# Three token tiles of a second product, cut into column and row parts of the array

## The chip, the cores and the metric

The kernel runs on one core of one Trainium2 chip. Its engines are TensorE (PE; PEld in the profile is its weight load), VectorE (DVE), ScalarE (ACT), GpSimd (POOL) and SyncE (SP, which here issues nearly all DMAs). The metric is device time in microseconds; less is better.

## The reference

The input x has 2048 tokens of 1024 features, in bf16. Each token is normalised over its features, multiplied by w1 (1024 x 3584), given a bias and a tanh GELU, and multiplied by w2 (3584 x 1024) with a second bias:

```python
def reference(x, w1, b1, w2, b2):
    y = _layernorm(x, axis=-1)
    h = _gelu(jnp.einsum("bsd,df->bsf", y, w1) + b1)
    return jnp.einsum("bsf,fd->bsd", h, w2) + b2
```

## The kernel before

All weights and all of x are kept in SBUF. The tokens are worked through in four blocks of 512 (`TB`), each of four token tiles of 128; tiles 4 to 7 are the second block, which the code calls block 1. For every block there are two products.

The first product (`mm1_row`, whose matmuls are issued by `pe_cell`, line 415) makes 28 rows of h, transposed: each row r has 128 of the 3584 hidden features on the partitions and the block's 512 tokens along the free dimension. A row is eight matmuls of 128x512, accumulated in one PSUM bank, followed by one GELU on ScalarE (line 432) into `hT_sb[:, r, :]`. The first block's opening rows are done in pieces of 128 tokens.

The second product (`out_chunk`, line 453) takes one token tile and one half of the 1024 output features at a time. Such a group is 28 matmuls (line 466), one for each `ft`. The stationary operand is a 128x128 square of `hT_sb` (128 hidden features by 128 tokens), the moving operand is 128x512 of `w2_sb`, and the 28 products accumulate in one bank of `ps_2`. That tensor has two banks (`NB2`), which the groups use in turn: group g waits until group g - 2 has been evicted (`grp_oe[g - NB2]`). The eviction is one addition on VectorE (line 477) which adds the bias `b2_sb` and writes bf16 to `o_sb`; then SP issues a store (line 482) of 128 KB. `o_sb` has two buffers, used by the token tiles in turn. Block 1 has eight groups, two to each of the tiles 4 to 7. The very last group of the kernel is cut into four pieces of 128 columns.

The order on each engine is that in which the program is written: every engine has a list of operations (`_Prog`), and `_emit` writes it out, with a wait on a semaphore only where the awaited value is higher than one the engine has already waited for. TensorE's list is strictly: first product of a block, second product of it, first product of the next.

VectorE's list is merged from two by a small planner (lines 569 to 584). `crit` holds the evictions, each with the time at which its matmuls are estimated to end; `fill` holds the preparation of the next blocks (statistics, normalisation, and the 32x32 stream transposes of line 355 that turn x into `yT_sb`). An eviction is taken when its estimated time has come, else a piece of preparation. The planner sets the order only; at run time each operation waits for its semaphores. The transposes that stand between the evictions of block 1 are those of block 3.

## Time and profile before

| what | value |
|---|---|
| timed runs | 398.50 and 398.64 us, median 398.57 |
| span of the profiled execution | 396.9 us (the page gives no total for it) |
| timed median less that span | 1.67 us |
| TensorE matmuls | 2116, busy 394.1 us |
| matmul of 128x512 in the second product | 868, mean 379 ns |
| weight load of 128x128 | mean 98 ns |
| VectorE busy | 152.8 us |
| eviction of 128x512 on VectorE | 31, mean 692 ns |

Matmuls are pipelined: the 379 ns run from the start of one to the modelled end of its drain, while the next has begun. The pace is read from start to start, by a stretch of the chain and the number of matmuls in it. The granted clock is the share of TensorE's full clock that the throttle let through.

The second product of block 1 by tiles, each a stretch from the first matmul of the tile to the first of the next:

| tile | stretch, us | TensorE busy | VectorE busy |
|---|---|---|---|
| 4 | 152.95 to 165.04 | 12.09 | 11.15 |
| 5 | 165.04 to 177.12 | 12.08 | 10.97 |
| 6 | 177.12 to 189.21 | 12.09 | 9.24 |
| 7 | 189.21 to 201.29 | 12.08 | 1.38 |

### The profile page before, as it was taken

To read this page: it belongs to the slowest core of one execution; us is meant where nothing else is said; L and a number is where in the kernel's file an instruction comes from. 1 tells how busy PE (TensorE), PEld (TensorE's weight loads), DVE (VectorE), ACT (ScalarE), POOL (GpSimd) and SP (SyncE) were. 2 spreads that over 40 slices of the span, in tenths; PEclk is the share of its full clock that TensorE was granted. 3 is DMA by queue.
4 is the path that set the end of the run, shared out by engine and by line. 5 is a ranking of instruction groups with operands and counts; after the bars stand their busy time and mean duration, and the time that the engine had idled before them with its cause. 6 is when DMAs were issued, how large, how long until landed. Compare 5 with 4: busy or idle time off the path is not lost.

```text
span 396.9 us, 4883 instructions
## 1 busy us (share of the span) xinstructions
PE 394.1 (99%) x2116; PEld 191.7 (48%) x2116; DVE 152.8 (38%) x345; ACT 82.8 (21%) x124; POOL 9.7 (2%) x24
## 2 busy tenths in 40 slices
PE   9999999999999999999999999999999999999998
PEld 8944444444444444444444444444444444444447
DVE  5847899989998005988100000001100000001011
ACT  4273430000133442000024433100003334400000
POOL 2101000020002000000000000000000000000000
PEclk9999999999999999999999999999999999999999
DMA  8999940000000000000000000000000000000000
GB/s 286 347 380 384 387 154 13 26 29 13 26 2 0 2 0 1 28 13 26 28 13 0 2 0 2 13 13 28 16 24 15 0 0 2 0 13 28 13 28 26
DMA packets 16924, 23.64 MB, mean 60 GB/s; under 512 B 1672, under 2 KB 10504, under 8 KB 16904
## 3 DMA queue, kind: packets, MB, share of 16 engines
q1 hardware_dynamic: 16616, 22.95, 16.4%
q8 instruction: 16, 0.26, 0.3%
q10 hardware_dynamic: 288, 0.39, 0.3%
q14 instruction: 4, 0.03, 0.0%
HBM read 19.14 MB, written 4.19 MB: 59 GB/s over the span
## 4 chain that ended last, share of the span: by engine, by line
PE 99%; ACT 0%; DVE 0%; issue 0%
PE ps L466 49%; PE ps L415 41%; PE ps_t L415 8%; PE ps L490 1%; PE ps_t L378 0%; ACT yT_sb L385 0%; DVE o_sb L477 0%
## 5 line engine op out<-in xcount | busy, mean ns | idle before, releaser
L466 PE MATMUL ps<-w_sb,hT_sb 128*128 128x512 bf16 (+1 forms) x980 | 194.2, 361 | 0.0
L415 PE MATMUL ps<-yT_sb,w_sb 128*128 128x512 bf16 (+1 forms) x920 | 167.4, 340 | 0.1
L466 PEld LDWEIGHTS ps<-w_sb,hT_sb 128*128 128x128 bf16 x980 | 91.3, 98 | 102.7
L415 PEld LDWEIGHTS ps<-yT_sb,w_sb 128*128 128x128 bf16 x920 | 80.9, 98 | 82.5 <-issue 0.3
L432 ACT ACTIVATE hT_sb<-ps,b_sb 128x512 bf16<-128x512 f32 x94 | 64.0, 688 | 237.2 <-PE ps L415 217.1
L477 DVE TENSOR_TENSOR o_sb<-ps,b_sb 128x512 bf16<-128x512 f32 (+1 forms) x35 | 22.6, 646 | 198.2 <-PE ps L466 198.1
L355 DVE STREAM_TRANSPOSE yT_sb<-x_sb 32x256 bf16<-32x256 bf16 x192 | 83.7, 436 | 26.6 <-PE ps_t L415 23.5
L415 PE MATMUL ps_t<-yT_sb,w_sb 128*128 128x512 bf16 x144 | 34.0, 379 | 0.0
L264 DVE BATCH_NORM_STATS2 st_sb<-x_sb 128x6 f32<-128x512 bf16 x32 | 21.1, 674 | 4.9 <-DMA x_sb<-in_x_dram 4.9
L415 PEld LDWEIGHTS ps_t<-yT_sb,w_sb 128*128 128x128 bf16 x144 | 14.0, 98 | 16.8
L432 ACT ACTIVATE hT_sb<-ps_t,b_sb 128x512 bf16<-128x512 f32 x18 | 12.4, 690 | 17.0 <-PE ps_t L415 14.6
L425 DVE TENSOR_TENSOR ps<-ps,rbc_sb 128x256 f32<-128x256 f32 x24 | 9.7, 426 | 6.1 <-PE ps L415 5.9
L268 POOL TENSOR_TENSOR rstd_sb<-mv_sb,nhalf 128x1 f32<-128x1 f32 x16 | 8.9, 559 | 118.7 <-DVE mv_sb L271 118.7
L290 DVE TENSOR_SCALAR x_sb<-x_sb,mv_sb,rstd_sb 128x1024 bf16<-128x1024 bf16 (+1 forms) x15 | 7.8, 525 | 3.9 <-POOL rstd_sb L268 3.3
L385 ACT COPY yT_sb<-ps_t 128x512 bf16<-128x512 bf16 (+2 forms) x8 | 4.4, 545 | 8.1 <-PE ps_t L378 8.1
L490 PE MATMUL ps<-const-bfloat16-1.0 128*128 128x128 bf16 x40 | 4.6, 302 | 0.8 <-PEq L613 0.8
L490 PEld LDWEIGHTS ps<-const-bfloat16-1.0 128*128 128x128 bf16 x40 | 4.0, 139 | 1.0 <-issue 0.8
L271 DVE BATCH_NORM_AGGREGATE mv_sb<-st_sb 128x2 f32<-128x15 f32 x16 | 3.5, 221 | 1.3
L337 DVE STREAM_TRANSPOSE rbc_sb<-rq_sb 32x64 f32<-32x64 f32 x16 | 3.8, 236 | 0.2
L378 PE MATMUL ps_t<-ident,x_sb 128*128 128x128 bf16 x24 | 2.3, 219 | 0.0
L425 DVE TENSOR_TENSOR ps_t<-ps_t,rbc_sb 128x256 f32<-128x256 f32 x4 | 1.6, 405 | 0.1
L493 ACT ACT_TABLE_LOAD x1 | 1.3, 1283 | 1.7 <-PEq L613 1.7
(24 smaller groups left out, 8.0 us busy)
## 6 DMA issues: line engine op xcount, KB each, us to landing
w_sb<-in_w_dram SPq DMA_DIRECT2D x4, 1792.0 KB, 18.3
out_dram<-o_sb SPq DMA_DIRECT2D x31, 128.0 KB, 1.7
x_sb<-in_x_dram SPq DMA_DIRECT2D x3, 1024.0 KB, 14.1
w_sb<-in_w_dram SPq DMA_DIRECT2D x2, 1024.0 KB, 9.1
w_sb<-in_w_dram SPq DMA_DIRECT2D x1, 2048.0 KB, 15.2
w_sb<-in_w_dram SPq DMA_DIRECT2D x8, 224.0 KB, 4.7
w_sb<-in_w_dram SPq DMA_DIRECT2D x1, 1280.0 KB, 14.7
x_sb<-in_x_dram SPq DMA_DIRECT2D x5, 128.0 KB, 4.6
```

The costliest lines, as they stand in the source:

```text
L264: return (lambda e, i=i, h=h: e.bn_stats(st_sb[:, i, 6 * h:6 * (h + 1)], x_sb[:, i, h * HC:(h + 1) * HC]), [x_ev[i][h]], f"st{i}_{h}", 0.65)
L268: pool.op(lambda e, i=i: e.tensor_tensor(out=rstd_sb[:, i:i + 1], in0=mv_sb[:, i, 1:2], in1=nhalf[:, i:i + 1], op=ALU.pow), waits=[f"mv{i} ...
L290: return (lambda e, i=i, c0=c0, c1=c1: e.tensor_scalar(out=x_sb[:, i, c0:c1], in0=x_sb[:, i, c0:c1], scalar1=mv_sb[:, i, 0:1], scalar2=rst ...
L337: res.append((lambda e, src=src, dst=dst: e.transpose(out=dst, in_=src), [f"rq{N_CENTRED - 1}"], ("rbc" if tq == 3 and q == 3 else None), ...
L355: res.append((lambda e, src=src, dst=dst: e.transpose(out=dst, in_=src), waits, (f"tr{i}" if lastop else None), 0.47))
L385: act.op(lambda e, dst=dst, src=src: e.copy(out=dst, in_=src), waits=[f"tp{i}_{k}"], sig=f"te{i}_{k}")
L415: pe.op(lambda e, b=b, r=r, dt=dt, n0=n0, n1=n1, bank=bank: e.matmul(unit_bank(bank)[:, n0:n1], lhsT=w1_sb[:, dt, r * P:(r + 1) * P], rhs= ...
L425: crit.append((est[wait_ev], (lambda e, ap=ap: e.tensor_tensor(out=ap, in0=ap, in1=rbc_sb[:, :, :].rearrange("p t s -> p (t s)"), op=ALU.m ...
L432: act.op(lambda e, r=r, n0=n0, n1=n1, bank=bank: e.activation(out=hT_sb[:, r, n0:n1], in_=unit_bank(bank)[:, n0:n1], func=ACT.Gelu_apprx_tanh,
L466: pe.op(lambda e, st=st, ft=ft, c0=c0, c1=c1, bank=bank: e.matmul(ps_2[:, bank, 0:c1 - c0], lhsT=hT_sb[:, ft, st * P:(st + 1) * P], rhs=w2 ...
L477: crit.append((est[sig], (lambda e, ob=ob, c0=c0, c1=c1, bank=bank: e.tensor_tensor(out=o_sb[:, ob, c0:c1], in0=ps_2[:, bank, 0:c1 - c0], ...
L490: pe.op(lambda e: e.matmul(ps_1[:, 0, 0:P], lhsT=unit, rhs=unit, start=True, stop=True), waits=[gate] if gate else [])
```

## The change

Three token tiles of block 1's second product are computed with their matmuls cut into parts; the other tiles are as before. `COL_SPLIT` and `ROW_SPLIT` name them.

In tile 4 (two column parts) and tile 5 (four), each of the 28 steps of a group becomes two or four matmuls. Each has 64 or 32 of the tile's tokens as stationary columns and so writes 64 or 32 partitions of the same PSUM bank; the moving operand is the same 128x512 of `w2_sb` every time.

In tile 6 (two row parts), each step becomes two matmuls, one over hidden features 0 to 63 of the 128 and one over 64 to 127. Each has 128 stationary columns and writes all 128 partitions, the first to the group's own bank and the second to the other bank of `ps_2`. The group therefore uses both banks, and it and the group after it wait for the eviction of the group just before (`grp_oe[g - 1]`). Its eviction is two additions on VectorE: own bank plus bias into a scratch `o32_sb` in fp32, then the other bank plus the scratch into `o_sb`. The parts of a step follow one another in TensorE's list.

```diff
+COL_SPLIT = {4: 2, 5: 4}
+ROW_SPLIT = {6: 2}
...
+        o32_sb = sb("o32_sb", [P, NCH], F32)
...
+            ncs, nrs = COL_SPLIT.get(ti, 1), ROW_SPLIT.get(ti, 1)
+            prev_ti = (g - 1) // DH
+            if g >= 1 and (nrs > 1 or prev_ti in ROW_SPLIT):
+                waits.append(grp_oe[g - 1])
+            mw, kw = P // ncs, P // nrs
             for ft in range(FT):
-                pe.op(lambda e, st=st, ft=ft, c0=c0, c1=c1, bank=bank: e.matmul(
-                    ps_2[:, bank, 0:c1 - c0], lhsT=hT_sb[:, ft, st * P:(st + 1) * P], rhs=w2_sb[:, ft, c0:c1],
-                    start=(ft == 0), stop=(ft == FT - 1)),
-                    waits=(waits if ft == 0 else []) + [hT_row[(b, ft)]],
-                    sig=(sig if ft == FT - 1 else None))
+                for q in range(ncs):
+                    for k in range(nrs):
+                        firstm, lastm = ft == 0 and q == 0 and k == 0, ft == FT - 1 and q == ncs - 1 and k == nrs - 1
+                        pe.op(lambda e, st=st, ft=ft, c0=c0, c1=c1, bk=(bank + k) % NB2, q=q, k=k, mw=mw, kw=kw: e.matmul(
+                            ps_2[q * mw:(q + 1) * mw, bk, 0:c1 - c0],
+                            lhsT=hT_sb[k * kw:(k + 1) * kw, ft, st * P + q * mw:st * P + (q + 1) * mw],
+                            rhs=w2_sb[k * kw:(k + 1) * kw, ft, c0:c1],
+                            start=(ft == 0), stop=(ft == FT - 1)),
+                            waits=(waits if firstm else []) + [hT_row[(b, ft)]],
+                            sig=(sig if lastm else None))
...
+            if nrs > 1:
+                crit.append((est[sig], (lambda e, ob=ob, c0=c0, c1=c1, bank=bank: e.tensor_tensor(
+                    out=o32_sb[:, :], in0=ps_2[:, bank, 0:c1 - c0], in1=b2_sb[:, c0:c1], op=ALU.add),
+                    list(dwaits), f"pp_{ti}_{c0}", 0.7), b))
+                crit.append((est[sig], (lambda e, ob=ob, c0=c0, c1=c1, bank=bank: e.tensor_tensor(
+                    out=o_sb[:, ob, c0:c1], in0=ps_2[:, 1 - bank, 0:c1 - c0], in1=o32_sb[:, :], op=ALU.add),
+                    [f"pp_{ti}_{c0}"], oe, 0.7), b))
+            else:
...
```

More of the change, by code (lines that the diff above doesn't have):

```diff
@@ L476, in out_chunk @@
             oe = f"oe_{ti}_{c0}"
-            crit.append((est[sig], (lambda e, ob=ob, c0=c0, c1=c1, bank=bank: e.tensor_tensor(
-                out=o_sb[:, ob, c0:c1], in0=ps_2[:, bank, 0:c1 - c0], in1=b2_sb[:, c0:c1], op=ALU.add),
-                dwaits, oe, 0.2 + (c1 - c0) * 1e-3), b))
+            if nrs > 1:
[6 more added lines that the diff above has]
+            else:
+                crit.append((est[sig], (lambda e, ob=ob, c0=c0, c1=c1, bank=bank: e.tensor_tensor(
+                    out=o_sb[:, ob, c0:c1], in0=ps_2[:, bank, 0:c1 - c0], in1=b2_sb[:, c0:c1], op=ALU.add),
+                    dwaits, oe, 0.2 + (c1 - c0) * 1e-3), b))
             grp_oe.append(oe)
```

## The prediction

> **What bounds the kernel now.** I read the page's busy shares first, then the chain that ended last, then TensorE's waits.

> ```profile
> PE 394.1 (99%) x2116; PEld 191.7 (48%) x2116; DVE 152.8 (38%) x345; ACT 82.8 (21%) x124; POOL 9.7 (2%) x24
> ...
> PE 99%; ACT 0%; DVE 0%; issue 0%
> ...
> PE ps L490 <- PEq L613: 0.8, 1, 0.8
> ```

> TensorE is busy 99% of the span, the chain is TensorE for 99%, and the waits (third line: of PE alone, total, times, longest) hold one entry, 0.8 us at the start. So any time added to TensorE's stream in the middle is added to the end; nothing downstream can absorb it. The changed stage is the second product of block 1, read from the chain in order of time and from the stretches of tiles 5 and 6:

> ```profile
> 153.12 48.35 PE ps L466 x224
> ...
> 165.04:177.12 12.08, 12.08 (x57) 5.49 (x56) 10.97 (x24) 0.00 (x0) 0.00 (x0) 1.00 0.06 22
> 177.12:189.21 12.09, 12.09 (x57) 5.49 (x56) 9.24 (x20) 0.00 (x0) 0.00 (x0) 1.00 0.06 22
> ```

> 224 matmuls (8 groups of 28) in 48.35 us: **215.8 ns** from one start to the next, 6.04 us a group, 12.08 a tile, at a granted clock of 1.00. The groups by shape give one matmul 379 ns, 163 more than that pace, so a matmul is still draining while the next streams. Weight loads (98 ns) lie inside the stream: PEld is busy 5.49 of 12.08 us.

> ```profile
> L466 PE MATMUL ps<-w_sb,hT_sb 128*128 128x512 bf16 x868 | 188.0, 379 | 0.0
> ...
> 8.72 3.41 PE ps L415 x61
> ```

> The second line, from the chain, is the first block's matmuls with 128 moving columns: a load and a matmul every 3.41/61 = **55.9 ns**, so a full load need not take more than that of the stream.

> **Part 1, the matmuls themselves.** Nothing is removed but the full-array form. Tile 4 goes from 56 matmuls to 112 (64 output columns each), tile 5 from 56 to 224 (32 each), tile 6 from 56 to 112 (64 contraction rows each). Every one still streams 512 columns. That is 280 matmuls and 280 loads more, with the same arithmetic. If the parts of one contraction step stream at the same time, a step costs one stream, 215.8 ns. If each part holds TensorE for its whole stream, the 280 cost 280 x 0.2158 = 60.4 us. [...] The nearest row by shape, the full 128x512 matmul, would price each at 215.8. I still take **0**: two parts of a step use other columns of the array (or other rows and another bank), need nothing of each other, and a matmul already waits neither for its predecessor's drain nor for its load's turn. This is an assumption, and it carries the forecast. [...]

> Loads and issue: four parts need four loads and four matmuls a step. By the 55.9 ns pair, two parts take 111.8 ns, hidden under 215.8; four take 223.6, which is 7.8 ns over. On tile 5's 56 steps: **+0.44 us**. Lower bound 0; the upper bound is the 98 ns load in a row, below.

> Changes of shape: full to two columns, two columns to four, four to rows, rows to full. The latter two fall into stalls counted below. For the first two I allow one drain each, 379 - 216 = 163 ns: **+0.33 us** (lower bound 0).

> **Part 2, the new waits.** A row-split group writes both PSUM banks, so it, and the group after it, must wait until the group just before is evicted; before, a group waited for the one two back, done 5 us earlier. Three such waits: ahead of tile 6's first half, of its second half, and of tile 7's first half. Behind them on TensorE's queue lies everything that follows, so each is paid in full. The price comes from these rows (column: start, duration, engine):

> ```profile
> 159.20 0.69 DVE L477 TENSOR_TENSOR o_sb<-ps,b_sb 128x512 bf16<-128x512 f32 x1 [0.22 <-PE ps L466]
> ...
> 120.42 1.29 DVE L264 BATCH_NORM_STATS2 st_sb<-x_sb 128x6 f32<-128x512 bf16 x2
> 121.81 0.22 DVE L271 BATCH_NORM_AGGREGATE mv_sb<-st_sb 128x2 f32<-128x15 f32 x1
> ...
> 5.40 0.38 ACT yT_sb L385
> 5.78 0.14 issue
> 5.92 0.49 PE ps L415 x6
> ```

> Group 0 of tile 4 starts at 152.95, so its 28 slots end at 158.99; its eviction starts at 159.20: 0.21 us of drain and signal. The eviction takes 0.69. TensorE, released by another engine, restarts 0.14 us after (last two lines, from the chain). First wait: 0.21 + 0.69 + 0.14 = **1.04 us**. A row-split group has two additions, the second waiting for the first on the same engine; the nearest such pair, statistics ending at 121.71 and aggregation starting at 121.81, leaves 0.10. I take 0.69 for each addition though their operands differ (fp32 scratch). Second and third wait: 0.21 + 0.69 + 0.10 + 0.69 + 0.14 = **1.83 us** each. Together **4.70 us**; without the 0.10 and with half the restart 4.3, and with a transpose in VectorE's way (436 ns) ahead of each eviction 6.0.

> I count no such transpose. VectorE does 11 transposes of a later block between two evictions and was idle 0.37 to 0.39 us before each of these; a TensorE that is late only lengthens that.

> ```profile
> 178.05 4.95 DVE L355 STREAM_TRANSPOSE yT_sb<-x_sb 32x256 bf16<-32x256 bf16 x11
> 183.37 0.69 DVE L477 TENSOR_TENSOR o_sb<-ps,b_sb 128x512 bf16<-128x512 f32 x1 [0.37 <-PE ps L466]
> ```

> The extra addition in the planner (0.7 + 0.7 against 0.71 us) may move a transpose or so behind tile 6; those transposes end at 187.2 and block 3's first product starts at 298.15, a cover of 110 us. Stores: the same eight on SP's queue, 1.7 us to land, their buffer used again two tiles (24 us) later. If those covers were gone each would cost its own lateness, but they are large. Extra PE instructions: tile 5 issues pairs at the rate of the 55.9 ns stretch, which ran without a gap, so I price their fetching at nothing.

> **Sum.** 4.70 + 0.33 + 0.44 = 5.47 us on the profiled span of 396.9, giving 402.4. The page gives no total for that execution; the two timed runs (median 398.57) lie 1.67 above the span, and I keep that distance: **404.0 us**, +1.4%. What a measurement of this kernel can tell from no change is about 2%, 8 us, so this counts as within.

> **Rivals.**

> A, the forecast, parts side by side: 402 to 406, chance 0.57.

> B, loads bound the four-column tile. If a part's load can only run after the part before has started, and its matmul after that load, a step is 4 x 98 = 392 ns, 176 over, 9.9 us on 56 steps in place of 0.44: 413.5. For it: loads always appear just one matmul ahead. Against: the 55.9 ns pair, which is shorter than one load. Partial forms lie between 406 and 413.5. Here too the pauses: the longest of TensorE now is 0.8 us, and the kernel's first 37 matmuls took 4.26 us, 115 ns each against 55.9. If each of three pauses brought 37 such back, that is 3 x 2.2 us: 410.6. Together 0.16.

> C, row parts one after the other, columns side by side: tile 6 +56 x 0.2158 = 12.1: 416.1. For it: both parts write all 128 partitions of PSUM, twice the usual writes. Chance 0.07.

> D, column parts one after the other (each needs its own 128-row stream of the same moving data), rows side by side: 56 + 168 matmuls, 48.3 us, without the 0.44: 451.9. Chance 0.06.

> E, **the slower side in full**: every part holds the array for its stream. Place: tiles 4, 5 and 6; price 60.4 us: 464.0. It decides early: the forecast leaves 2.5 us to the 2% bound, so 8.9 ns of each extra matmul's 215.8 is enough. For it: every 512-column matmul of this trace takes its 215.8. Chance 0.09.

> F, column loads not even beside a stream: 215.8 + 98 for each of 336 column matmuls, 105.4 us where 24.2 were, so 81.3 more: 484.9. Chance 0.03. [...] The trace speaks against it as it stands, since full loads lie inside streams of the same rows here.

> G, not slower than before: the change doing less than it says, the parts merged or the waits already over. The waits' events are new and the eviction can't start before the group ends, so 4.3 us stand against it; 398.6, chance 0.02.

> **Range and chances.** A, B and C hold 0.80; the range goes from 401.5 (stalls at their lower price, no drains) to 417. D, E, F and G, 0.20, are left out. Within 2% (up to 406.5): A, G's not-slower case and B's lowest edge, 0.58; slower 0.41; faster 0.01.

> **What would show it.** Right: stretches of about 12.1 us for tile 4, 12.5 for tile 5, 15.0 for tile 6 with the waits ahead of its halves and 13.9 for tile 7 with its own, TensorE waiting for VectorE three times, 1.0, 1.8 and 1.8 us, and the rest of the trace shifted by about 5.5 us. B shows in tile 5 alone (near 22 us); C in tile 6 at some 27; D and E in tile 4 at 24 and tile 5 at 48; F in tile 4 at 35. The forecast is wrong if the parts do not share time, above all for columns, of which this trace says nothing.

## The result, and the profile after

The changed kernel takes 404.49 us (404.22 and 404.76) against 398.57, a ratio of 1.0151 with a 95% interval of 1.0132 to 1.0170: 5.9 us or 1.5% slower, inside the 2% that the prediction called no change, at 0.5 us from the forecast of 404.0. The profiled execution took 404.76 us, of which 403.5 are the span.

First the waits of TensorE in the changed kernel (total us, times, longest), of which the kernel before had none in the middle:

```profile
PE ps L477 <- DVE o_sb L494: 3.3, 2, 1.7
PE ps L477 <- DVE o_sb L498: 0.9, 1, 0.9
```

L477 is now the matmul of the second product, L498 the single addition of an eviction, L491 and L494 the two additions after row parts. Three waits, two long and one short, as many as the change added. Next the chain of the changed kernel through block 1's second product (start, duration, what):

```profile
153.37 24.44 PE ps L477 x336
177.80 0.02 issue
177.83 0.70 DVE o_sb L498
178.53 0.14 issue
178.66 6.23 PE ps L477 x56
184.90 0.02 issue
184.92 0.70 DVE o_sb L491
185.62 0.02 issue
185.65 0.70 DVE o_sb L494
186.35 0.05 issue
186.40 6.24 PE ps L477 x56
192.63 0.02 issue
192.66 0.70 DVE o_sb L491
193.36 0.02 issue
193.38 0.70 DVE o_sb L494
194.08 0.27 issue
194.35 10.74 PE ps L477 x49
205.09 0.05 issue
205.15 1.24 PE ps L477 x5
206.39 8.63 PE ps L418 x40
```

The first line holds tiles 4 and 5: 112 + 224 matmuls in 24.44 us, where 112 whole ones had taken 2 x 12.08 = 24.16 (the last one's drain is in the 24.44). So the parts do share the time. From 177.80 on, the five additions of three evictions stand in the chain, with TensorE idle; before, evictions lay beside matmuls. The 0.27 at 194.08 is not a longer restart: that group's weight loads begin at 194.12, and its eviction comes 6.03 us after its first recorded matmul, 6.26 after that in the two groups before. One matmul's record is missing there, and TensorE restarted some 0.06 us after the addition. The stage runs from 153.37 to 206.39, **53.02 us against 48.35: +4.67**. The stretches by tile, from first matmul to first matmul (length, then busy time and count by engine, PE first):

```profile
153.29:165.38 12.09, 12.09 (x113) 6.26 (x112) 11.15 (x25) 0.69 (x1) 0.00 (x0) 1.00 0.04 13
165.38:177.60 12.22, 12.22 (x226) 5.85 (x224) 10.97 (x24) 0.00 (x0) 0.00 (x0) 1.00 0.07 24
```

Tile 4 has twice and tile 5 four times the matmuls of before in the same 12.1 to 12.2 us. Matmul by matmul, the trace has four parts of a step starting 2 to 5 ns apart and the next step 216 ns after the first of them.

The evictions give the price of each group, since they start at its end (from rounded times; a 0.01 is rounding):

| eviction starts at | of group | after the one before | over 6.04 |
|---|---|---|---|
| 159.57, 165.62 | tile 4 | (first), 6.05 | 0.01 |
| 171.78, 177.83 | tile 5 | 6.16, 6.05 | 0.12, 0.01 |
| 184.92, 192.66 | tile 6 | 7.09, 7.74 | 1.05, 1.70 |
| 200.38, 206.43 | tile 7 | 7.72, 6.05 | 1.68, 0.01 |

The first eviction comes 6.20 us after the stage begins, before it was 6.08: 0.12 more. So the stage's 4.67 are 4.43 of waits and 0.24 at the two changes of shape that no wait hides, within 0.04.

The stage does not account for everything. The last eviction starts at 400.02 instead of 395.10, 4.92 later: 0.25 come from the head, where an input transfer landed 0.27 us later. That is scatter: over the profiles of this case the last matmul before the stage starts between 152.74 and 153.34. The other part is behind it: from the start of the last eviction to the end of the span it is 3.5 us instead of 1.8. SP's own wait for the last store shows it, in the kernel before and then in the changed one:

```profile
SPq L78 <- DMA out_dram<-o_sb: 0.9, 1, 0.9
```

```profile
SPq L80 <- DMA out_dram<-o_sb: 2.6, 1, 2.6
```

In the trace's DMA records a packet of 16 KB from the instruction queue starts at 401.07 and takes 1.21 us, until 402.28. Of the last store's 144 packets 135 end by 401.45, and nine run from 402.27 to 402.54. Nine of 144 is what one of 16 DMA engines would carry of a store spread evenly, so the fetch seems to have held that one; this is concluded from the count, the records don't name the engine. In long stretches of whole matmuls such packets come some 27.6 us apart, the time of 128 matmuls and their 128 loads, and in tile 5, with eight instructions a step, they start at 169.55 and 176.56, 7.01 us apart where 32 steps take 6.91; so I take them to bring TensorE's instructions, 256 at a time. The pages count 16 before and 19 after:

```profile
q8 instruction: 16, 0.26, 0.3%
```

```profile
q8 instruction: 19, 0.31, 0.3%
```

### The profile page after: what moved, and what is told of

It reads as the page before. It is cut to its first block, busy times and chain, and to the rows that moved or that the text cites. A ratio compares the mean times of both kernels' runs of the same rounds, so it can differ in the third digit from the quotient of the medians.

```text
span 403.5 us, 5414 instructions
## 1 busy us (share of the span) xinstructions
PE 393.1 (97%) x2364; PEld 193.0 (48%) x2396; DVE 154.5 (38%) x347; ACT 83.0 (21%) x124; POOL 9.8 (2%) x24
## 4 chain that ended last, share of the span: by engine, by line
PE 96%; DVE 1%; DMA 1%; issue 1%; ACT 0%; DVEq 0%
PE ps L477 48%; PE ps L418 40%; PE ps_t L418 8%; DMA x_sb<-in_x_dram 1%; PE ps_t L381 0%; DVE o_sb L491 0%; DVE o_sb L494 0%; DVE o_sb L498 0%; ACT o_sb L515 0%; PE ps L511 0%; PE ps L381 0%; DVE m_sb L278 0%; DVEq L80 0%
## 5 line engine op out<-in xcount | busy, mean ns | idle before, releaser
L477 PE MATMUL ps<-w_sb,hT_sb 128*128 128x512 bf16 (+4 forms) x1245 | 194.0, 364 | 4.9 <-DVE o_sb L494 3.3
L477 PEld LDWEIGHTS ps<-w_sb,hT_sb 128*128 128x128 bf16 (+3 forms) x1260 | 92.5, 98 | 106.0 <-DVE o_sb L494 4.0
L498 DVE TENSOR_TENSOR o_sb<-ps,b_sb 128x512 bf16<-128x512 f32 (+1 forms) x33 | 21.2, 643 | 196.8 <-PE ps L477 196.7
L271 POOL TENSOR_TENSOR rstd_sb<-mv_sb,nhalf 128x1 f32<-128x1 f32 x16 | 9.0, 561 | 118.9 <-DVE mv_sb L274 118.9
L491 DVE TENSOR_TENSOR o_sb<-ps,b_sb 128x512 f32<-128x512 f32 x2 | 1.4, 692 | 4.6 <-PE ps L477 4.6
## 6 DMA issues: line engine op xcount, KB each, us to landing
w_sb<-in_w_dram SPq DMA_DIRECT2D x4, 1792.0 KB, 18.3
```

The costliest lines, as they stand in the source:

```text
L271: pool.op(lambda e, i=i: e.tensor_tensor(out=rstd_sb[:, i:i + 1], in0=mv_sb[:, i, 1:2], in1=nhalf[:, i:i + 1], op=ALU.pow), waits=[f"mv{i} ...
L477: pe.op(lambda e, st=st, ft=ft, c0=c0, c1=c1, bk=(bank + k) % NB2, q=q, k=k, mw=mw, kw=kw: e.matmul(ps_2[q * mw:(q + 1) * mw, bk, 0:c1 - c ...
L498: crit.append((est[sig], (lambda e, ob=ob, c0=c0, c1=c1, bank=bank: e.tensor_tensor(out=o_sb[:, ob, c0:c1], in0=ps_2[:, bank, 0:c1 - c0], ...
```

## The experiments

The theory at this point: parts of a step stream side by side at no cost, the waits cost 4.4 us, a change of shape 0.1 us, and some 1.1 us at the end belong to an instruction fetch. The rivals are named with each run. Edits are against the changed kernel.

### Columns only, and rows only

```diff
-ROW_SPLIT = {6: 2}
+ROW_SPLIT = {}
```

> Tiles 4 and 5 in column parts, tile 6 whole. Theory (parts of a step stream side by side; only a change of shape costs): tile 4 and tile 5 about 12.1 to 12.2 us each, the stage of 224 steps 0.2 to 0.3 us longer than the 48.35 of before, no wait of TensorE for VectorE, time 398.7 to 399.1. Rival (the columns cost part of the 5.9 us, by slower loads): tile 5 clearly above 12.2 us, time above 400.

Measured: 398.74 us, ratio 1.0007 (0.9998 to 1.0016) on 398.45, so +0.29 and hardly to be told from nothing. The evictions of tile 5 lie 6.17 and 6.04 us apart, and TensorE waits for no eviction. The columns are free but for three changes of shape, 0.09 to 0.12 us each.

```diff
-COL_SPLIT = {4: 2, 5: 4}
+COL_SPLIT = {}
```

> Tile 6 in row parts, tiles 4 and 5 whole. Theory: three waits for evictions of 1.05, 1.70 and 1.68 us beyond a group's 6.04, together 4.4, and nothing else: the stage 52.8 us, time 403.0. The tail after the last eviction as in the kernel before (1.5 us), since the instruction fetch that falls into the changed kernel's last store falls elsewhere. Rival (the whole 5.9 us belongs to the rows): 404.5.

Measured: 403.03 us, ratio 1.0119 (1.0104 to 1.0135): +4.58. Evictions lie 7.09, 7.74 and 7.72 us apart, SP waits 0.9 us for the last store, and TensorE's waits are those of the changed kernel:

```profile
PE ps L477 <- DVE o_sb L494: 3.3, 2, 1.7
PE ps L477 <- DVE o_sb L498: 0.9, 1, 0.9
```

The rows carry the stage's loss, but not all 5.9 us.

### Rows without the waits

The second row part goes to one of two banks of the first product, which are idle during the second, and the scratch gets two buffers:

```diff
-COL_SPLIT = {4: 2, 5: 4}
+COL_SPLIT = {}
...
-        o32_sb = sb("o32_sb", [P, NCH], F32)
+        o32_sb = sb("o32_sb", [P, 2, NCH], F32)
...
-            if g >= 1 and (nrs > 1 or prev_ti in ROW_SPLIT):
-                waits.append(grp_oe[g - 1])
+            if nrs > 1:
+                waits.append(bank_gelu[("1", g % 2)])
...
-                            ps_2[q * mw:(q + 1) * mw, bk, 0:c1 - c0],
+                            bk[q * mw:(q + 1) * mw, 0:c1 - c0],
...
+                bank_gelu[("1", g % 2)] = oe
```

Here `bk` is `ps_2[:, bank]` for the first part and `ps_1[:, g % 2]` for the second.

> Tile 6 in row parts as in the rows-only run, but its second part goes to a bank of the first product, idle then, so that no group waits for the one just before. Theory (the waits are the whole price of the rows): no wait of TensorE for VectorE, evictions again 6.04 to 6.15 us apart, stage within 0.3 us of 48.35, time 398.6 to 399.0. Rival (two row parts writing two banks at once are slower by themselves, or their drain costs): over 399.5.

Measured, with tile 6 alone split: 398.63 us, ratio 1.0004 (0.9995 to 1.0013). The evictions of that run, from (5, second half) to (6, second half):

```profile
177.65 0.69 DVE L497 TENSOR_TENSOR o_sb<-ps,b_sb 128x512 bf16<-128x512 f32 x1 [0.39 <-PE ps L476]
183.81 0.69 DVE L490 TENSOR_TENSOR o_sb<-ps,b_sb 128x512 f32<-128x512 f32 x1 [0.49 <-PE ps L476]
184.53 0.69 DVE L493 TENSOR_TENSOR o_sb<-ps,o_sb 128x512 bf16<-128x512 f32 x1
189.85 0.69 DVE L490 TENSOR_TENSOR o_sb<-ps,b_sb 128x512 f32<-128x512 f32 x1 [1.45 <-PE ps L476]
```

6.16 and 6.04 us apart, with both additions still there. So the price of the rows was the bank, not the second addition and not the writing of two banks.

### Parts in every tile

```diff
-COL_SPLIT = {4: 2, 5: 4}
-ROW_SPLIT = {6: 2}
+COL_SPLIT = {i: 4 for i in range(15)}
+ROW_SPLIT = {}
```

> Four column parts in tiles 0 to 14 instead of tile 5, no row parts: 840 steps in four parts, so that a price per step shows. Theory (no price per step; one change of shape into and out of each block's second product, 0.1 us each): 399 to 400. Rival (the predicted 7.8 ns a step, loads and issue just over the stream): 840 x 7.8 ns = 6.6 us, 405. Rival (instruction fetches, doubled in rate, fall behind): gaps in TensorE's stream with nobody waited for, over 405.

Measured: 399.36 us, ratio 1.0023 (1.0014 to 1.0033), +0.91. Block 1's second product is one piece in its chain, 896 matmuls in 48.46 us against 224 in 48.35:

```profile
153.60 48.46 PE ps L477 x896
```

840 steps in four parts and eight changes of shape (into and out of each block's second product) cost 0.91 us together, 0.11 a change with nothing left for the steps. The 7.8 ns a step, 6.6 us, are refuted.

The same with rows, on the spare-bank kernel:

```diff
-ROW_SPLIT = {6: 2}
+ROW_SPLIT = {i: 2 for i in range(15)}
```

> Two row parts with a spare bank for the second in tiles 0 to 14: 840 steps in two parts and 30 more additions on VectorE. Theory (no price per step, no wait): 398.6 to 400, the extra additions (21 us on VectorE in all) hidden. Rival (a price per step of a few ns from writing two banks): 3 ns would be 2.5 us, 401. Rival (the doubled evictions make VectorE late in blocks 0 and 1, where transposes fill it): TensorE waits for VectorE there, over 400.

Measured: 399.29 us, ratio 1.0022 (1.0013 to 1.0032), +0.84, eight changes again. Thirty more additions (VectorE 174.1 us busy against 153) made nobody wait.

### The parts apart

```diff
-            for ft in range(FT):
-                for q in range(ncs):
-                    for k in range(nrs):
+            for q in range(ncs):
+                for k in range(nrs):
+                    for ft in range(FT):
```

> The changed kernel's instructions in another order: in tiles 4, 5 and 6 all 28 steps of one part come first, then all of the next, so that no two parts of a step stand next to each other. Same matmuls, loads, waits and evictions. Theory (parts run side by side only where the next matmul in the list uses other columns or rows): each matmul takes its own 216 ns: tile 4 24.2 us, tile 5 48.4, tile 6 24.2 and its pauses, +60.4 on the changed kernel, time some 464 to 465. Rival (a narrow matmul is cheaper by itself, whatever its neighbour): 404 to 406.

Measured, in one run: 464.34 us. The total is the expected one, but by accident: the tiles are not. Evictions of tile 5's two halves in the trace's order of time:

```profile
196.93 0.69 DVE L498 TENSOR_TENSOR o_sb<-ps,b_sb 128x512 bf16<-128x512 f32 x1 [16.06 <-PE ps L477]
217.72 0.69 DVE L498 TENSOR_TENSOR o_sb<-ps,b_sb 128x512 bf16<-128x512 f32 x1 [15.13 <-PE ps L477]
```

20.8 us for 112 matmuls where 112 x 0.2158 = 24.2 was expected, and 10.42 for tile 4's second half where it was 12.1. The starts in the trace say why: 24 starts come alone, 216 ns apart, then four pairs with two starts within 5 to 30 ns each, then 20 alone, four pairs, and so on. By the count of 28 to a part, the first four matmuls of the next part run beside the last four of the one before. 112 less four overlaps of four is 96, and 96 x 0.2158 = 20.7. Tile 6 went the other way. Its two groups and the start of tile 7, as stretches; the third number from the right is the granted clock:

```profile
218.50:230.00 11.50, 11.40 (x56) 4.88 (x56) 4.74 (x12) 0.00 (x0) 0.00 (x0) 1.00 0.03 11
231.40:251.50 20.10, 19.96 (x56) 6.88 (x56) 3.11 (x9) 0.00 (x0) 0.00 (x0) 0.56 0.02 7
252.90:265.00 12.10, 12.06 (x45) 4.98 (x46) 0.69 (x1) 0.00 (x0) 0.00 (x0) 0.80 0.07 23
```

The clock was halved from 233.9 to 257.8, and a matmul then took 427 ns from start to start. What stands: apart from these overlaps each narrow matmul took its full 216 ns at full clock, and the order in the list is what made the parts share time.

The same order for rows alone, on the spare-bank kernel:

```diff
-ROW_SPLIT = {6: 2}
+ROW_SPLIT = {5: 2, 6: 2}
```

> Two row parts in tiles 5 and 6, all 28 steps of one part ahead of the other's, with the spare bank, so without any pause: four groups of 56 matmuls of 64 rows, of which four in a group's middle overlap. Theory (the halved clock of the parts-apart run came from 64-row matmuls alone on the array, not from the pauses): the granted clock falls to a half some 10 to 20 us into the tiles and stays there until some 5 us of whole matmuls have run; time well over the 421 that 24 + 24 us for the two tiles give. Rival (the pauses did it): granted clock 1.00 throughout, tiles 5 and 6 some 22 to 24 us each, time 418 to 422.

Measured, in one run: 416.98 us. This run's trace holds no record of the granted clock, but its starts are 216 ns apart throughout the two tiles, where half the clock made them 427. Evictions are 10.40 us apart (48 slots: 56 less two overlaps of four; I had counted one, so the time lies just below the rival's 418):

```profile
187.32 0.69 DVE L490 TENSOR_TENSOR o_sb<-ps,b_sb 128x512 f32<-128x512 f32 x1 [4.47 <-PE ps L476]
197.72 0.69 DVE L490 TENSOR_TENSOR o_sb<-ps,b_sb 128x512 f32<-128x512 f32 x1 [4.45 <-PE ps L476]
```

My theory falls: 42 us of 64-row matmuls alone did not halve the clock here. In the parts-apart run they had pauses, 1.3 and 1.9 us from start to start; the changed kernel has such pauses between side-by-side parts and kept its clock (1.00). So of the three, only the run with both lost it. But that run also had 64 us of narrow column matmuls, one at a time, ahead of them, and no run tells these apart from the pauses. What halved it is left open.

### The change of shape

Tile 5 alone, every other step in four parts and the others whole:

```diff
-COL_SPLIT = {4: 2, 5: 4}
-ROW_SPLIT = {6: 2}
+COL_SPLIT = {5: 4}
+ROW_SPLIT = {}
...
+                ncs = COL_SPLIT.get(ti, 1) if ft % 2 else 1
+                mw = P // ncs
```

> Tile 5 alone, with every other step in four column parts and the steps between whole: 28 parted and 28 whole steps, 55 changes of shape inside the tile and two at its ends, no row parts. Theory (a change of shape costs about 0.1 us, as at the two visible changes of the changed kernel): tile 5 17.2 to 18.3 us, time about 404 to 405. Rival (a change costs the full drain of 163 ns that was predicted): tile 5 21.0 us, time 407.5. Rival (a change costs nothing; the 0.1 us was the wait for the eviction or chance): 398.7.

Measured, in one run: 405.02 us, +6.57. From the last eviction of tile 4 to that of tile 5 and the first of tile 6:

```profile
165.84 0.69 DVE L500 TENSOR_TENSOR o_sb<-ps,b_sb 128x512 bf16<-128x512 f32 x1 [0.37 <-PE ps L479]
174.88 0.69 DVE L500 TENSOR_TENSOR o_sb<-ps,b_sb 128x512 bf16<-128x512 f32 x1 [3.36 <-PE ps L479]
184.00 0.69 DVE L500 TENSOR_TENSOR o_sb<-ps,b_sb 128x512 bf16<-128x512 f32 x1 [3.47 <-PE ps L479]
190.14 0.69 DVE L500 TENSOR_TENSOR o_sb<-ps,b_sb 128x512 bf16<-128x512 f32 x1 [0.46 <-PE ps L479]
```

Tile 5 takes 18.16 us, 6.08 over 12.08, and the next group 0.10 over its 6.04: 6.18 us for 56 changes (the tile begins with a whole step, so one end has none), **0.110 us each**. The drain of 163 ns is too much, and nothing is too little.

### The end of the kernel

Small matmuls whose result nobody reads are put into the pauses; the output is unchanged.

```diff
+            if g in (13, 14):
+                warm(20)
```

> The changed kernel with 20 small matmuls (128x128, 56 ns each) put into the second and the third pause of TensorE, 1.1 us of work in pauses of some 1.7: 80 TensorE instructions more, output unchanged. Theory (in the changed kernel a 16 KB instruction fetch holds one DMA engine just when the last store comes, 1.1 us): the fetches come 80 instructions sooner against the end, some 2.2 us, and miss the last store, so the time after the last eviction falls from 3.2 to about 1.5 to 2.1 us in the profile, and the time from 404.5 to about 403.3. Rival (the tail's length is chance, or the pauses are not idle): the time stays at 404.5 or rises by up to 2.2.

Measured: 403.17 us (403.06 to 403.41), with SP's last wait at 0.9 us. The last fetch starts at 397.10, 3.0 us ahead of the last eviction.

> The changed kernel once more, beside the one with four fillers. Theory (an instruction fetch in the way of the last store, fixed by the number of TensorE instructions): time 404.2 to 404.8 again, in the profile a last store that SP waits 2.6 us for, and a 16 KB instruction packet starting about 1.0 us after the last eviction begins. Rival (the long tail was chance): 403.0 to 403.4, a wait of 0.9 us.

This is the changed kernel without an edit; beside it ran one with fewer fillers:

```diff
+            if g == 13:
+                warm(4)
```

> The changed kernel with 4 small matmuls (8 TensorE instructions) in the second pause, where the run with 40 had them too. Theory: the last fetch starts 0.2 to 0.6 us sooner against the end, still over the last store but by less: SP's wait for the last store between 1.2 and 2.5 us, time 403.5 to 404.3, between the changed kernel and the run with 40 fillers (403.17). Rival (fillers speed things up by something else in the pauses, such as a warm array): 403.2, or no change at 404.5.

Measured, on one chip: the changed kernel again 404.38 us (404.27 to 404.79), with four fillers 403.25 (402.96 to 403.39). So eight instructions more take 1.1 us away, all that 80 took; the partial gain that I expected of so few did not come. The last fetch moved from behind the last eviction to 399.06, a microsecond ahead of it. The second profile of the changed kernel does not show what I expected either: its last fetch starts at 403.26, after the last store's packets have ended (401.54), SP's wait is 0.9 us and the span 401.9, and yet that execution took 404.31 us, 2.4 over its span where every other execution takes 1.2 to 1.4. So the 1.1 us come with a last fetch that falls behind the work, in the way of the store or after it. The fillers did not speed up the work itself: the last eviction starts at 400.09 with four of them and at 400.12 without. In the twelve other profiles of this case, those with fillers among them, the last fetch starts ahead of the last eviction, and none shows the extra time. That the fetch is what costs it is concluded from this; where it holds the time when it comes after the store, no trace shows.

### Short streams

```diff
-COL_SPLIT = {4: 2, 5: 4}
-ROW_SPLIT = {6: 2}
+COL_SPLIT = {15: 4}
+ROW_SPLIT = {}
```

> Four column parts in tile 15 alone, no row parts. Its first group has 512 moving columns, its second is cut into four pieces of 128 moving columns, so there a step of 55.9 ns has eight instructions instead of two: the point where loads and issue could show. Theory (parts share the time down to short streams): pieces 1.57 us each as before, time 398.7. Rival (a load and a matmul take some 28 ns each to issue, as 55.9 ns a pair would have it): a step 223.6 ns, pieces 6.3 us each, time 417. Between the two, the pace gives what a part costs.

Measured, in one run: 403.51 us, between the two. A step of the short pieces keeps its 56 ns with eight instructions (first group of the pieces: starts at 389.19, 389.24, 389.30), so loads and issue cost nothing even here. Then TensorE stops three times, waiting for nothing that the profile shows. From the chain of that run (start, duration, what):

```profile
391.87 0.96 issue
392.83 1.97 PE ps L477 x128
394.80 1.48 issue
396.28 1.97 PE ps L477 x128
398.25 1.76 issue
400.01 0.41 PE ps L477 x14
```

It runs 128 matmuls and their 128 loads and stops, and in the trace's DMA records the fetches of 16 KB start at 390.50, 393.87 and 397.32, 3.4 us apart, and TensorE resumes 2.3 to 2.7 us after each start. The four pieces need 896 instructions in 6.3 us, and the fetches brought 256 in 3.4.

No run was faster than the kernel before; the best variants, columns only and rows with a spare bank, are level with it.

## Why the prediction was right

The forecast was 5.47 us over the kernel before; 5.92 were measured. By its own steps:

- **What bounds the kernel.** Right: what was added to TensorE's stage was added to the end, 4.67 us in the stage and 4.67 of the last eviction's 4.92, the rest being the head.
- **The matmuls themselves at 0.** Right, and the assumption it rested on is now shown: side by side a step of two or four column parts or of two row parts takes 216 ns, over 56 steps and, for four columns and two rows, over 840; apart, each part takes it. Rivals C, D and E fell with it, and G with the waits. Rival F fell too: the column parts' loads (110 and 97 ns) lie beside streams of the same rows, in tile 5 5.85 us of loads in the 12.22 us in which TensorE was busy throughout. In these long accumulations four column parts took the slot of one (224 matmuls in 12.22 us, where 56 whole ones took 12.08), and so did two row parts (56 in 6.23 us, where 28 took 6.04; 0.16 of it is the last drain, 379 less 216 ns).
- **Loads and issue, +0.44.** Wrong step, small: tile 5's second half took its 6.04 us as before, and 840 steps show nothing either. The 55.9 ns pair was not set by a load and an issue in turn; the short-stream run shows four loads and four matmuls within 56 ns. B, which priced loads at 98 ns in a row, fell with it. Its other half, slow matmuls after each pause, did not come either: after the three pauses the starts are 215 to 226 ns apart.
- **Changes of shape, +0.33.** Mis-sized: 0.12 each instead of 0.163, so 0.24 for two; over 56 changes the mean is 0.110.
- **The waits, +4.70.** Right in number, place and order: 1.05, 1.70 and 1.68, together 4.43, against 1.04, 1.83 and 1.83. The two additions follow one another after 0.03 us, not the 0.10 taken from another pair, and the restart after a wait was 0.14 only the first time, then 0.05 and some 0.06. The addition with other operands took 0.69 as assumed. The spare-bank run, +0.18 us, shows that these waits are the price of the rows, but for changes of shape.
- **No transpose in VectorE's way.** Right: VectorE was idle 0.39, 1.43 and 3.14 us before the three evictions.
- **Extra instructions, fetched at nothing.** Wrong. The rate was no problem in tile 5, but with 560 more TensorE instructions the last 16 KB fetch started at 401.07, behind the last eviction at 400.02 (before: 385.57, ahead of 395.10); eight more, which moved it ahead again, took 1.1 us away (404.38 against 403.25). It is a step that the prediction named and priced at 0 by looking at the stage alone.

So the total came out so well in part because two errors cancelled: 0.8 us too much in the stage, 1.1 us missing at the end. 4.67 + 1.13 on the 398.48 of the same chip's runs is 404.28, where 404.38 was measured. The span alone was forecast less well, 402.4 against 403.5. The 1.67 us kept between span and time made that good: the profiled execution took 1.26 over its span, and the kernel before takes 1.2 to 1.4 over its own in the later runs, so the 396.9 was probably a quicker execution's than the two timed ones.

One bound of the forecast does not follow from its terms: stalls at their lower price of 4.3 us and nothing else give 402.9 on 398.57, not 401.5. The measured time does not depend on it.

## What to carry to other kernels

Cutting a matmul into column or row parts of the array cost TensorE nothing here as long as the parts of a step stood next to each other in its list; the same matmuls in another order cost 60 us more (464.34 against 404.49), some of it by the halved clock. What has to be priced is what comes along: the bank that a row part takes from the double buffering (1.1 to 1.7 us a group, nothing with a spare bank), 0.11 us a change of shape, and the longer instruction stream, which stalled the short streams of the last tile for 4.2 us and put a fetch at the end of the kernel (1.1 us). Where a stage has been priced from its rows and a microsecond is still missing, look at the tail of the span, and at the time beyond it.
